# Fused attention and maxout feed-forward on one core: ScalarE's exponential moved ahead of evictions and of the rounding of value products, reciprocals moved within VectorE's order

## The chip, the cores and the metric

One NeuronCore of one Trainium2 chip runs the whole kernel. The metric is the device time of one execution in microseconds, lower is better. The engines are TensorE (PE, with its weight loads as PEld), VectorE (DVE), ScalarE (ACT), GpSimd (POOL) and SyncE (SP, which issues most transfers). Each runs its own instructions in program order and waits on semaphores for the others.

## What is computed

Causal attention with a learned decay, then a maxout feed-forward block (B = 8, H = 8, S = 576, D = 64, 4608 tokens, model width 512, inner width 768):

```python
scores = scale * np.matmul(q, k.transpose(0, 1, 3, 2))
cum = np.cumsum(np.maximum(s, 0.0), axis=-1)
bias = -(cum[:, :, :, None] - cum[:, :, None, :])
scores = np.where(causal, -1000000000.0, scores + np.minimum(bias, 0.0))
scores = scores - np.max(scores, axis=-1, keepdims=True)
attn = np.exp(scores)
attn = attn / (np.sum(attn, axis=-1, keepdims=True) + 1e-09)
x = (attn @ v) ...            # to 4608 x 512
h = np.maximum(np.maximum(x @ w1, x @ w2), x @ w3)
out = h @ w_out
```

## The kernel before

Operands of the large products are kept as a high and a low half (f16 pairs, or rounded f32 pairs for q and k), so each rounding takes two steps: ScalarE writes the high half (`prh` for the probabilities, `xh` for the value products), VectorE subtracts it from the exact value and writes the low half (`prl`, `xl`).

The attention is cut into visits, one for a batch and a pair of heads. The first two batches are visited twice, for query blocks 0 and 1 and then for 2, 3 and 4; every later batch has one visit of five blocks per pair of heads (a stacked visit). A step t is one block of 128 queries of one visit; there are 160. The order of all work is written by hand in the loop at L941, and each engine keeps to it. For step t that loop issues, in this order:

- `probs(t)`, first part: the reciprocal `ri` of the sums (L513, VectorE), then `prh` (L529, ScalarE);
- `highest(t+1)`: the negated row maximum `nm` of the next step's scores (L469 or L474, VectorE);
- `probs(t)`, second part: `prl` (L532, VectorE) and the transposes of both halves (by transfers at L541 and L548, or on TensorE in the first visits);
- `drain()` and `flush()`, then one feed-forward group if one is due (`run_group`);
- `scores(t+2)` on TensorE, into the buffer of step t: there are two score buffers, so `prh` and `prl` of step t must have read theirs;
- `expo(t+1)`: two exponentials with sums (L484) and the scaled sum `se` (L489), ScalarE;
- `drain()` and `flush()` again, then the step's list `todo` of preparatory work (on VectorE the splits L162 and L338, maxima of values L300, low halves of values L362 and of weights L704), more feed-forward groups, and `values` of a finished half of a visit (products `av`, L608).

`pending` holds work that follows a product of TensorE. `out` (in `values`) rounds a value product: L617 on ScalarE and L618 on VectorE. The `ev` of a feed-forward group evicts it: of three groups `pm` (L731, twelve matmuls each) the first goes through ScalarE (L745), the others through VectorE (L748), which take the maximum. The output groups `po` (L773) go through ScalarE (L781), scaled by `os` (L766). `flush` issues GpSimd's split of the result into `hh` and `hl`. When the last pair of heads of a batch is rounded, `add_set` queues the groups of a feed-forward set; how many groups a step issues is set by a running account of TensorE's time (`cost`).

```python
next(parts)
drain()
flush()
if ready() and cost[0] > 0:
    run_group()
...
if t + 1 < len(steps):
    expo(t + 1)
```

Of the kernel before, what the change touches and what calls it, by code (L numbers as in the profile page):

```python
# [8 lines left out]
F32 = mybir.dt.float32  # L9
# [6 lines left out]
ALU = mybir.AluOpType  # L16
# [5 lines left out]
def kernel(  # L22
# [9 lines left out]
    nc = tc.nc  # L32

    P = 128
# [9 lines left out]
    NFT = NW // 4  # L44
    NB = qkv0.shape[0]
# [248 lines left out]
    AM, VS, OS = {}, {}, {}  # L294
# [183 lines left out]
    def expo(t):  # L478
# [11 lines left out]
        SE[t] = (se, nj)  # L490

    PT = {}
    TP = {}
# [6 lines left out]
    def probs(t):  # L500
# [10 lines left out]
        pT = PT[v, ph]  # L511
        ri = small.tile([P, 2], F32, tag="ri", name=f"ri{t}", bufs=3)
        nc.vector.reciprocal(out=ri[:, :nj], in_=se[:, :nj])  # L513
        halves = [att.tile([P, 8, P], F16, tag=f"pr{c}", name=f"pr{c}{t}") for c in "hl"]
# [197 lines left out]

    def drain():
        while pending:
            pending.pop(0)()

    def add_set(b, ph):
# [5 lines left out]

        def h_group(ft, i):
            pm = ps_m.tile([P, 512], F32, tag="m", name=f"pm{u}_{ft}_{i}")
            w = W[3 * ft + i]
# [34 lines left out]
        def o_group(dt):  # L761
            drain()
            flush()
            if dt == 0:
                st["os"] = small.tile([P, 1], F32, tag="os", name=f"os{u}", bufs=2)
                nc.gpsimd.tensor_scalar(  # L766
                    out=st["os"], in0=OS[b, ph if b < NB else 1], scalar1=WS["kw"], scalar2=None, op0=ALU.mult
                )
            pm = ps_m.tile([P, 512], F32, tag="m", name=f"po{u}_{dt}")
# [24 lines left out]
    def flush():  # L794
        while later:
            later.pop(0)()

    def ready():
        return bool(queue) and all(i in W for i in queue[0][1])
# [24 lines left out]

    early = {}

    def soon(t, f, *a):
        early.setdefault(t, []).append((f, a))

    middle = {}  # L830
# [104 lines left out]
    scores(1)  # L935
    expo(0)
    for t in sorted(k for k in todo if k < 0):
        for f, a in todo[t]:
            if f not in (prep2, prep3) or a[0] > 1:
                f(*a)  # L940
    for t, (v, qb) in enumerate(steps):  # L941
# [11 lines left out]
        next(parts)  # L953
        drain()
        flush()
        if ready() and cost[0] > 0:
            run_group()
        for f, a in early.get(t, ()):
            f(*a)
        if t + 2 < len(steps):  # L960
# [7 lines left out]
        for f, a in todo.get(t, ()):  # L968
            f(*a)
        while ready() and cost[0] > 0:  # L970
            run_group()
# [66 lines left out]
```

## Time and profile before

| what | value |
|---|---|
| median of 3 runs (lowest, highest) | 893.19 us (892.27, 893.97) |
| the profiled execution's own time | 893.29 us |
| its span on the engines | 891.5 us |
| TensorE busy, idle | 831.3 us (93%), 60.2 us |
| VectorE busy | 582.6 us (65%) |
| ScalarE busy | 558.9 us (63%) |
| GpSimd busy | 369.3 us (41%) |

The span goes from the first to the last instruction; the 1.8 us between it and the execution's time lie around it. An engine's idle time matters only where another engine, in the end TensorE, waits for it. The waits and the timeline name for an idle stretch the engine and line that ended it.

### The profile page before, as it was taken

To read this page: it belongs to the slowest core of one execution; us is meant where nothing else is said; L and a number is where in the kernel's file an instruction comes from. 1 tells how busy PE (TensorE), PEld (TensorE's weight loads), DVE (VectorE), ACT (ScalarE), POOL (GpSimd) and SP (SyncE) were. 2 spreads that over 40 slices of the span, in tenths; PEclk is the share of its full clock that TensorE was granted. 3 is DMA by queue.
4 is the path that set the end of the run, shared out by engine and by line. 5 is a ranking of instruction groups with operands and counts; after the bars stand their busy time and mean duration, and the time that the engine had idled before them with its cause. 6 is when DMAs were issued, how large, how long until landed. Compare 5 with 4: busy or idle time off the path is not lost. (4 is left out here: it accounts for less than half of the span.)

```text
span 891.5 us, 19856 instructions
## 1 busy us (share of the span) xinstructions
PE 831.3 (93%) x7048; PEld 647.5 (73%) x7048; DVE 582.6 (65%) x1465; ACT 558.9 (63%) x1486; POOL 369.3 (41%) x580
## 2 busy tenths in 40 slices
PE   4878889889999879999999999999999999999998
PEld 2646678766677668777787778877887778777875
DVE  6778877567677667676776767676767676661110
ACT  4567676566677766776768766666767676751111
POOL 5533424223636525455463534455454535221211
PEclk9999999989999979999999999999999999999999
DMA  9722355565986675776767656666657586541000
GB/s 358 271 74 56 100 130 142 132 145 131 195 179 145 162 154 112 165 145 137 167 144 161 148 150 160 154 139 144 160 118 154 144 153 126 94 73 39 13 13 30
DMA packets 233588, 120.75 MB, mean 135 GB/s; under 512 B 209361, under 2 KB 218065, under 8 KB 233489
## 3 DMA queue, kind: packets, MB, share of 16 engines
q1 hardware_dynamic: 232336, 117.65, 56.5%
q10 hardware_dynamic: 1152, 1.84, 0.7%
q8 instruction: 56, 0.92, 0.5%
q14 instruction: 44, 0.35, 0.2%
HBM read 60.18 MB, written 9.44 MB: 78 GB/s over the span
## 5 line engine op out<-in xcount | busy, mean ns | idle before, releaser
L731 PE MATMUL pm<-x,w 128*128 128x256 f16 (+1 forms) x3456 | 453.1, 288 | 3.0 <-DVE x L618 2.1
L731 PEld LDWEIGHTS <-w 128*128 128x128 f16 x3456 | 330.3, 99 | 95.0 <-issue 9.6
L737 POOL CAST hh<-m 128x256 f16<-128x256 f32 (+1 forms) x96 | 54.9, 572 | 347.3 <-DVE m L748 293.8
L529 ACT ACTIVATE prh<-s,ri 128x512 f16<-128x512 f32 (+3 forms) x288 | 142.1, 539 | 84.3 <-DVE ri L513 78.6
L532 DVE SCALAR_TENSOR_TENSOR prl<-s,ri,prh 128x512 f16<-128x512 f32 (+3 forms) x288 | 152.9, 568 | 50.0 <-ACT prh L529 34.9
L748 DVE SCALAR_TENSOR_TENSOR m<-pm,m 128x256 f32<-128x256 f32 (+1 forms) x192 | 87.3, 455 | 134.6 <-PE pm L731 117.4
L484 ACT ACTIVATE s<-s,nm 128x512 f32<-128x512 f32 (+4 forms) x288 | 151.2, 525 | 11.9 <-DVE nm L469 5.0
L773 PE MATMUL po<-hh,w 128*128 128x256 f16 (+1 forms) x768 | 148.9, 286 | 2.2 <-POOL hh L737 2.2
L773 PEld LDWEIGHTS <-w 128*128 128x128 f16 x1152 | 110.1, 98 | 35.1 <-issue 7.3
L469 DVE CUSTOM_DVE_ANT_0 s<-s,later 128x128 f32<-128x128 f32 (+1 forms) x192 | 94.5, 492 | 30.2 <-PE s L391 26.9
L773 PE MATMUL po<-hl,w 128*128 128x320 f16 (+1 forms) x384 | 109.7, 286 | 2.0 <-POOL hl L738 1.9
L745 ACT ACTIVATE m<-pm 128x256 f32<-128x256 f32 (+1 forms) x96 | 39.2, 408 | 92.3 <-PE pm L731 91.8
L738 POOL TENSOR_TENSOR hl<-m,hh 128x256 f16<-128x256 f32 (+1 forms) x96 | 74.8, 779 | 7.8
L781 ACT ACTIVATE o<-po,os 128x256 f32<-128x256 f32 (+1 forms) x64 | 31.9, 499 | 70.1 <-PE po L773 57.5
L171 POOL TENSOR_TENSOR l<-raw,h 64x576 fp32r<-64x576 f32 x48 | 67.8, 1413 | 13.1 <-ACT h L157 11.6
L474 DVE TENSOR_REDUCE nm<-s 128x1 f32<-128x576 f32 (+3 forms) x64 | 49.9, 779 | 23.8 <-PE s L433 9.6
L140 POOL CAST l<-kb 64x576 fp32r<-64x576 f32 x48 | 33.0, 688 | 74.3 <-PE s L402 68.7
L391 PE MATMUL s<-h 128*128 128x128 f32 (+1 forms) x192 | 54.9, 368 | 7.6 <-ACT se L489 2.6
L608 PEld LDWEIGHTS <-vh 128*64 128x64 f16 x832 | 47.5, 116 | 19.0 <-issue 11.6
L484 ACT ACTIVATION_READ_ACCUMULATOR s<-s,nm 128x1 f32 x288 | 57.3, 199 | 0.0
L608 PE MATMUL av<-ph,vh 128*64 128x320 f16 (+3 forms) x384 | 53.6, 296 | 0.3 <-DMA ph<-prh 0.3
L617 ACT ACTIVATE x<-av 128x256 f16<-128x256 f32 (+1 forms) x64 | 26.2, 410 | 36.9 <-PE av L608 35.6
(145 smaller groups left out, 1091.3 us busy)
## 6 DMA issues: line engine op xcount, KB each, us to landing
raw<-in_qk_dram SPq DMA_DIRECT2D x48, 608.0 KB, 4.6
r<-in_w_dram SPq DMA_DIRECT2D x24, 512.0 KB, 10.2
rv<-in_qkv_dram SPq DMA_DIRECT2D x32, 320.0 KB, 3.2
out_dram<-o SPq DMA_DIRECT2D x32, 160.0 KB, 2.0
out_dram<-o SPq DMA_DIRECT2D x32, 128.0 KB, 2.1
raw<-in_qkv_dram SPq DMA_DIRECT2D x8, 480.0 KB, 3.8
ph<-prh SPq DMA_TRANSPOSE x184, 2.9
pl<-prl SPq DMA_TRANSPOSE x184, 2.6
```

What stands on the lines that cost most here:

```text
L171: nc.gpsimd.tensor_tensor(out=l[far, QP:V0], in0=raw[far, QP:V0], in1=h[far, QP:V0].bitcast(F32), op=ALU.subtract)
L391: nc.tensor.matmul(ps[:, j, :nk], lhsT=w[:, qs], rhs=w[:, QP:QP + nk], start=(x == "h"), stop=(x == "l"), skip_group_check=True,)
L469: nc.vector.tensor_tensor_reduce(out=sc[:, j], in0=sc[:, j], in1=future[0][:, Q4 - nk:Q4], scale=-1.0, scalar=3.0e38, op0=ALU.add, op1=ALU ...
L484: nc.scalar.activation(out=sc, in_=sc, func=AF.Exp, bias=nm[:, j:j + 1], scale=-1.0 if below(t) else 1.0, accum_out=sm[:, j:j + 1],)
L529: nc.scalar.activation(out=hi, in_=src, func=AF.Copy, scale=sc)
L532: nc.vector.scalar_tensor_tensor(out=lo, in0=src, scalar=sc, in1=hi, op0=ALU.mult, op1=ALU.subtract)
L608: nc.tensor.matmul(av[j * D:(j + 1) * D, c0:nq], lhsT=lt, rhs=rt, start=(n < 2), stop=(n >= len(todo) - 2), skip_group_check=True,)
L731: nc.tensor.matmul(pm[:, :nq], lhsT=w[:, wt, kt, :], rhs=xt, start=(n == 0), stop=(n == 3 * NKT - 1))
L737: nc.gpsimd.tensor_copy(out=st["hh"][:, ft, :nq], in_=m1[:, :nq])
L738: nc.gpsimd.tensor_tensor(out=st["hl"][:, ft, :nq], in0=m1[:, :nq], in1=st["hh"][:, ft, :nq], op=ALU.subtract)
L748: nc.vector.scalar_tensor_tensor(out=m1[:, :nq], in0=pm[:, :nq], scalar=HSC, in1=m1[:, :nq], op0=ALU.mult, op1=ALU.max)
L773: nc.tensor.matmul(pm[:, :nq], lhsT=W[18 + ft][:, wt, dt, :], rhs=st[ht][:, ft, :nq], start=(n == 0), stop=(n == 3 * NFT - 1),)
```

## The change

`drain` gets an argument, how many entries to leave, and stops at an `out`. The drain ahead of `scores(t+2)` and `expo(t+1)` leaves the last eviction and each `out` in `pending`, and the flush there is gone; both are issued by the drain behind `expo(t+1)`. The reciprocal leaves `probs`: a new function `inverse(t+1)` issues it in step t, behind the first entry of `todo` that works on VectorE (`on_vector`), or behind the whole list. The scale `os` is computed with the last feed-forward group of a set rather than with the first output group, and only the first output group drains and flushes. An unused list (`early`, `soon`) goes.

```diff
+    RI = {}
+    def inverse(t):
+        se, nj = SE[t]
+        RI[t] = small.tile([P, 2], F32, tag="ri", name=f"ri{t}", bufs=3)
+        nc.vector.reciprocal(out=RI[t][:, :nj], in_=se[:, :nj])
...
-        ri = small.tile([P, 2], F32, tag="ri", name=f"ri{t}", bufs=3)
-        nc.vector.reciprocal(out=ri[:, :nj], in_=se[:, :nj])
+        ri = RI.pop(t)
...
-    def drain():
-        while pending:
+    def drain(left=0):
+        while len(pending) > left and not (left and pending[0].__name__ == "out"):
             pending.pop(0)()
...
         def h_group(ft, i):
+            if (ft, i) == (NFT - 1, 0):
+                st["os"] = small.tile([P, 1], F32, tag="os", name=f"os{u}", bufs=2)
+                nc.gpsimd.tensor_scalar(
+                    out=st["os"], in0=OS[b, ph if b < NB else 1], scalar1=WS["kw"], scalar2=None, op0=ALU.mult
+                )
...
         def o_group(dt):
-            drain()
-            flush()
             if dt == 0:
-                st["os"] = small.tile([P, 1], F32, tag="os", name=f"os{u}", bufs=2)
...
+                drain()
+                flush()
...
+    on_vector = (vmax, vscale2, prep3, prep5, head_qlo, decode2, decode4, gram2, wscale2)
...
     expo(0)
+    inverse(0)
...
         next(parts)
-        drain()
-        flush()
+        drain(1 + sum(f.__name__ == "out" for f in pending))
         if ready() and cost[0] > 0:
             run_group()
...
         for f, a in todo.get(t, ()):
             f(*a)
+            if f in on_vector and t + 1 < len(steps) and t + 1 not in RI:
+                inverse(t + 1)
+        if t + 1 < len(steps) and t + 1 not in RI:
+            inverse(t + 1)
```

What this does to the order of each engine, at three places. In the rows of the changed kernel the lines behind the edit have other numbers: L535 is L529 of before, L538 is L532, L623 and L624 are L617 and L618, L742 is L731, L756 and L759 are L745 and L748; the reciprocal (L513) is L497.

ScalarE, steps 46 to 48 (a stacked visit's query blocks 1 to 3; `x16_1` is the rounded second value product of the visit before, `pm1_1_3_0` a feed-forward group). Before:

```order
L529 ACTIVATE prh46_3897<-s46_3780,ri46_3895 128x2x128 x2
L617 ACTIVATE x16_1_3907<-av16_1_3866 128x320
L484 ACTIVATE s47_3842,sm47_3929<-s47_3842,nm47_3843 128x384 x2
L489 ACTIVATE se47_3932<-sm47_3929 128x2
L157 ACTIVATE h18_1_3859<-raw18_1_3719 128x576
L529 ACTIVATE prh47_3957<-s47_3842,ri47_3955 128x3x128 x2
L745 ACTIVATE m11_1_3_3967<-pm1_1_3_0_3940 128x320
L484 ACTIVATE s48_3923,sm48_3993<-s48_3923,nm48_3924 128x512 x2
L489 ACTIVATE se48_3996<-sm48_3993 128x2
```

and with the change:

```order
L535 ACTIVATE prh46_3897<-s46_3779,ri46_3855 128x2x128 x2
L484 ACTIVATE s47_3840,sm47_3926<-s47_3840,nm47_3841 128x384 x2
L489 ACTIVATE se47_3929<-sm47_3926 128x2
L623 ACTIVATE x16_1_3931<-av16_1_3868 128x320
L157 ACTIVATE h18_1_3861<-raw18_1_3719 128x576
L535 ACTIVATE prh47_3957<-s47_3840,ri47_3940 128x3x128 x2
L484 ACTIVATE s48_3920,sm48_3991<-s48_3920,nm48_3921 128x512 x2
L489 ACTIVATE se48_3994<-sm48_3991 128x2
L756 ACTIVATE m11_1_3_3996<-pm1_1_3_0_3942 128x320
```

The rounding `x16_1` stood between `prh46` and the exponential of step 47 and now stands behind that exponential; the eviction of the first group of three moved from ahead of the exponential of step 48 to behind it. Of the 63 roundings that stood between a `prh` and the next exponential, 61 moved like this one.

TensorE, the first feed-forward set (`av3_0` is the last value product that the set needs, `pm0_0_0_0` to `_2` its first three groups, `s10` the scores of a step two ahead, `gmv1_0` a small product for the next values' scale; of each run of equal matmuls one or two rows are shown). Before:

```order
L608 MATMUL av3_0_834<-pl6_717,vh3_691 64x128
L731 MATMUL pm0_0_0_0_863<-x0_0_433,w0_779 128x256
L427 MATMUL s10_876<-qkh5_768 128x128 x2
L433 MATMUL s10_876<-tri_99,identb_98 128x128
L291 MATMUL gmv1_0_902<-identb_98,ambv1_0_900 128x128
L731 MATMUL pm0_0_0_1_915<-x0_0_433,w0_779 128x256
L731 MATMUL pm0_0_0_2_928<-x0_0_433,w1_782 128x256
```

and with the change:

```order
L614 MATMUL av3_0_836<-pl6_719,vh3_693 64x128
L427 MATMUL s10_861<-qkh5_770 128x128 x2
L433 MATMUL s10_861<-tri_99,identb_98 128x128
L291 MATMUL gmv1_0_889<-identb_98,ambv1_0_887 128x128
L742 MATMUL pm0_0_0_0_902<-x0_0_452,w0_781 128x256
L742 MATMUL pm0_0_0_1_915<-x0_0_452,w0_781 128x256
L742 MATMUL pm0_0_0_2_928<-x0_0_452,w1_784 128x256
```

The first group stood ahead of the scores and now stands behind them and behind the small product. The same happens at three later sets.

VectorE, steps 20 and 21 (`qkl10` is a split of the queries and keys of a later visit). Before:

```order
L362 SCALAR_TENSOR_TENSOR vl9_1831<-rv9_1116,inv0_1_1763,vh9_1830 128x640
L338 SCALAR_TENSOR_TENSOR qkl10_1918<-raw10_1590,qkh10_1838 128x384
L513 RECIPROCAL ri20_1952<-se20_1910 128x2
L474 TENSOR_REDUCE nm21_1897<-s21_1896 128x1
L532 SCALAR_TENSOR_TENSOR prl20_1955<-s20_1808,ri20_1952,prh20_1954 128x4x128 x2
L618 SCALAR_TENSOR_TENSOR x8_1_1963<-av8_1_1923,x8_1_1963 128x320
```

and with the change:

```order
L362 SCALAR_TENSOR_TENSOR vl9_1831<-rv9_1118,inv0_1_1748,vh9_1830 128x640
L497 RECIPROCAL ri20_1916<-se20_1909 128x2
L338 SCALAR_TENSOR_TENSOR qkl10_1920<-raw10_1590,qkh10_1840 128x384
L474 TENSOR_REDUCE nm21_1896<-s21_1895 128x1
L538 SCALAR_TENSOR_TENSOR prl20_1955<-s20_1807,ri20_1916,prh20_1954 128x4x128 x2
L624 SCALAR_TENSOR_TENSOR x8_1_1992<-av8_1_1925,x8_1_1992 128x320
```

The reciprocal of step 20 stood behind the split and now stands ahead of it. In 32 of the 160 steps the reciprocal moves in such a way, in the others it stays where it was.

## Rows read from the trace of the kernel before

**Rows 1.** The profile's page, its part on busy time: microseconds, share of the span and number of instructions of each engine.

```profile
PE 831.3 (93%) x7048; PEld 647.5 (73%) x7048; DVE 582.6 (65%) x1465; ACT 558.9 (63%) x1486; POOL 369.3 (41%) x580
```

**Rows 2.** Busy time by stretch of the span: the stretch, its length, then busy time (and instructions) of PE, PEld, DVE, ACT and POOL, the granted clock of TensorE (1.00 is full), the DMA engines' share and GB/s.

```profile
340.00:880.00 540.00, 532.35 (x4619) 421.75 (x4616) 337.59 (x902) 334.58 (x894) 230.48 (x369) 1.00 0.57 124
```

**Rows 3.** All waits of the execution, by the engine and line that waited and what released it: total microseconds, times, the longest.

```profile
DVE m L748 <- PE pm L731: 117.4, 90, 11.7
ACT m L745 <- PE pm L731: 91.8, 58, 4.5
...
ACT x L617 <- PE av L608: 35.6, 35, 4.6
...
PE s L427 <- DVE prl L532: 6.4, 3, 3.4
...
PE s L402 <- DVE prl L532: 5.6, 6, 3.2
...
PE pm L731 <- DVE x L618: 2.1, 3, 0.8
```

**Rows 4.** Groups of instructions of ScalarE by line and shape: count | busy microseconds, mean nanoseconds of one | idle time before them.

```profile
L484 ACT ACTIVATION_READ_ACCUMULATOR s<-s,nm 128x1 f32 x288 | 57.3, 199 | 0.0
...
L484 ACT ACTIVATE s<-s,nm 128x384 f32<-128x384 f32 x64 | 35.5, 554 | 1.4 <-DVE nm L474 0.2
...
L489 ACT ACTIVATE se<-sm 128x2 f32<-128x2 f32 x128 | 26.1, 204 | 4.1
```

**Rows 5.** The timeline of one step of a stacked visit (the first such visit, its query blocks 1 to 4): start, duration, engine, line, what it does, in brackets the idle time before it and what ended it.

```profile
272.06 0.44 ACT L617 ACTIVATE x<-av 128x320 f16<-128x320 f32 x1
272.33 0.14 DVE L469 DVE_READ_ACCUMULATOR2_ANT nm<- 128x1 f32 x1
...
272.51 0.56 ACT L484 ACTIVATE s<-s,nm 128x384 f32<-128x384 f32 x1
...
273.12 0.48 DVE L618 SCALAR_TENSOR_TENSOR x<-av,x 128x320 f16<-128x320 f32 x1
...
273.78 0.49 DVE L748 SCALAR_TENSOR_TENSOR m<-pm,m 128x320 f32<-128x320 f32 x1 [0.18 <-PE pm L731]
...
274.31 0.82 DVE L162 SCALAR_TENSOR_TENSOR h<-raw,h 64x640 fp32r<-64x640 f32 x1
...
274.51 3.43 PE L731 MATMUL pm<-x,w 128*128 128x320 f16 x24
...
275.24 0.68 DVE L469 CUSTOM_DVE_ANT_0 s<-s,later 128x512 f32<-128x512 f32 x1
...
276.63 1.14 DVE L532 SCALAR_TENSOR_TENSOR prl<-s,ri,prh 128x384 f16<-128x384 f32 x2
...
277.92 0.48 PE L402 MATMUL s<-h 128*128 128x256 f32 x2
```

**Rows 6.** The timeline of the same step in the last such visit, same columns.

```profile
692.08 0.48 DVE L618 SCALAR_TENSOR_TENSOR x<-av,x 128x320 f16<-128x320 f32 x1
...
693.90 0.70 DVE L469 CUSTOM_DVE_ANT_0 s<-s,later 128x512 f32<-128x512 f32 x1 [0.30 <-PE s L391]
...
695.31 1.14 DVE L532 SCALAR_TENSOR_TENSOR prl<-s,ri,prh 128x384 f16<-128x384 f32 x2
...
696.87 0.51 PE L402 MATMUL s<-h 128*128 128x256 f32 x2
```

**Rows 7.** The timeline around the first feed-forward set, same columns.

```profile
64.55 2.23 PE L731 MATMUL pm<-x,w 128*128 128x256 f16 x10
...
66.62 0.61 DVE L532 SCALAR_TENSOR_TENSOR prl<-s,ri,prh 128x128 f16<-128x128 f32 x2
...
67.14 0.42 DVE L618 SCALAR_TENSOR_TENSOR x<-av,x 128x256 f16<-128x256 f32 x1
...
67.61 0.38 PE L731 MATMUL pm<-x,w 128*128 128x256 f16 x2 [0.84 <-DVE x L618]
...
69.86 0.25 PE L291 MATMUL gmv<-identb,ambv 128*128 128x128 bf16 x1 [1.06 <-DVE ambv L287]
```

**Rows 8.** Busy time by stretch at the same place, columns as in rows 2.

```profile
66.50:69.90 3.40, 1.50 (x15) 0.87 (x14) 3.37 (x11) 3.05 (x10) 0.00 (x0) 1.00 0.17 39
70.00:73.30 3.30, 3.30 (x17) 2.33 (x16) 2.09 (x5) 2.69 (x9) 0.00 (x0) 0.50 0.41 109
```

**Rows 9.** The timeline around the fourth feed-forward set, columns as in rows 5.

```profile
326.09 1.26 PE L731 MATMUL pm<-x,w 128*128 128x256 f16 x10
...
326.21 1.41 DVE L532 SCALAR_TENSOR_TENSOR prl<-s,ri,prh 128x512 f16<-128x512 f32 x2 [0.28 <-ACT prh L529]
...
328.00 0.38 PE L731 MATMUL pm<-x,w 128*128 128x256 f16 x2 [0.65 <-DVE x L618]
```

**Rows 10.** Single rows of the timeline at three other places where TensorE waits or a chain is late, same columns.

```profile
101.87 0.88 DVE L532 SCALAR_TENSOR_TENSOR prl<-s,ri,prh 128x256 f16<-128x256 f32 x2 [0.58 <-ACT prh L529]
...
102.89 0.39 PE L427 MATMUL s<-qkh 64*128 64x256 f32 x2 [3.40 <-DVE prl L532]
...
139.47 1.41 DVE L532 SCALAR_TENSOR_TENSOR prl<-s,ri,prh 128x512 f16<-128x512 f32 x2 [0.68 <-ACT prh L529]
...
159.63 0.38 ACT L745 ACTIVATE m<-pm 128x256 f32<-128x256 f32 x1 [1.70 <-PE pm L731]
...
164.19 1.14 DVE L532 SCALAR_TENSOR_TENSOR prl<-s,ri,prh 128x384 f16<-128x384 f32 x2 [0.75 <-ACT prh L529]
```

More of the change, by code (lines that the diff above doesn't have):

```diff
@@ L761, in o_group @@
         def o_group(dt):
-            drain()
-            flush()
             if dt == 0:
-                st["os"] = small.tile([P, 1], F32, tag="os", name=f"os{u}", bufs=2)
-                nc.gpsimd.tensor_scalar(
-                    out=st["os"], in0=OS[b, ph if b < NB else 1], scalar1=WS["kw"], scalar2=None, op0=ALU.mult
-                )
+                drain()
+                flush()
             pm = ps_m.tile([P, 512], F32, tag="m", name=f"po{u}_{dt}")
@@ L823 @@
     todo = {}
-    early = {}
-    def soon(t, f, *a):
-        early.setdefault(t, []).append((f, a))
+    on_vector = (vmax, vscale2, prep3, prep5, head_qlo, decode2, decode4, gram2, wscale2)
     middle = {}
@@ L953 @@
         next(parts)
-        drain()
-        flush()
+        drain(1 + sum(f.__name__ == "out" for f in pending))
         if ready() and cost[0] > 0:
             run_group()
-        for f, a in early.get(t, ()):
-            f(*a)
         if t + 2 < len(steps):
```

## The prediction, made before the changed kernel ran

> **What bounds the kernel now.** I read the page's busy times first, then the stretches, then the waits, then the timeline of the places that the waits name. TensorE is busy 93% of the span, VectorE 65% and ScalarE 63% [rows 1]. After 340 us TensorE works 532.35 of 540 us at the full granted clock [rows 2]; before that it stands still here and there. So a microsecond counts only if TensorE loses or gains it. ScalarE waits long for TensorE ahead of an eviction (91.8 us at L745) and ahead of a rounding of value products (35.6 us at L617), and in program order the next exponential stands behind both; that is what the change attacks. But TensorE itself waits for the chain of scores, maximum, exponential, reciprocal, `prh`, `prl` only 6.4 + 5.6 = 12.0 us in all [rows 3]. That is all there is to win on this chain.
>
> Times are reckoned against the profiled run, 893.29 us, of which the span is 891.5. The median of the three runs is 893.19, 0.1 us less.
>
> **What moves, and the rule of its cost.** TensorE may write the scores of step t+2 only when `prl` of step t, on VectorE, has read the buffer. VectorE runs in program order. Of the change only two things reach it: the reciprocal moves in 32 of 160 steps, and the second half of a rounding (L618) must wait until ScalarE has done the first half (L617), which now comes after the exponential. Where VectorE reaches L618 before that, all behind it waits too: evictions, split, the next maximum, the next `prl`.
>
> *Steady part, loss.* The exponential of a 128x384 block takes 2 x 0.554 on ScalarE, 2 x 0.199 for the sums and 0.204 for the scaled sum, some 1.6 us with the starts [rows 4]. In the step shown, ScalarE ran L617 at 272.06, while VectorE was still at the maximum, whose last part ended at 272.33 + 0.14 = 272.47; the exponential followed at 272.51 [rows 5]. So L617 sat in a hole: moving it lets the exponential start 0.04 sooner, nothing more. Now L617 starts at about 274.06 and ends 0.44 later, at 274.5. L618 ran at 273.12, so it comes 1.4 late. Of that the wait of 0.18 ahead of the eviction at 273.78 is absorbed, and from there VectorE has no idle time up to `prl` at 276.63: eviction, split, reciprocal and maximum stand end to end. `prl` ends at 277.77 + 1.2, and the scores, which started at 277.92, 0.15 after it (0.14 stands between the two at 102.89 too, where TensorE did wait for `prl` [rows 10], so it isn't slack), come 1.2 late: **+1.2**. TensorE has no other work in its program order there: the 24 matmuls ahead end at 277.94 [rows 5].
>
> In the last such step L618 at 692.08 comes 1.4 late, the maximum at 693.90 had waited 0.30 for scores and other small idle time takes 0.1, so `prl` comes 1.0 late; its end, 696.45, left 0.28 of slack beyond the 0.14 until the scores at 696.87: +0.7 [rows 6]. I did this at every rounding. Ten of the stacked visits lose, the first and the last as shown, the others between 0.1 and 1.1: together **+5.8**. At the other roundings of the stacked part TensorE finished the value products so late that L618 had waited for L617 anyway, or VectorE waits for TensorE behind it; there I cost the move at nothing. If that cover (117.4 us of VectorE waiting for groups of L731 [rows 3]) were thinner, each would cost up to the same 1.2; if the 0.14 and 0.15 were slack, the ten would cost 4.3.
>
> *First groups of the sets.* In three sets the first group, whose last two matmuls need the last rounding, waited for it 2.1 us in all [rows 3]. That group now stands behind the scores of t+2. At the first set 2.23 us of it ran from 64.55 while `prl` (66.62, 0.61) was still to come. Now TensorE idles from 64.6 until the scores can start at 67.4, and again, behind the scores, until the small product L291 at 69.86, which comes some 0.9 later, since VectorE gets to L618 0.9 later (ScalarE's exponential first) [rows 7]. Idle time grows from 0.84 + 1.06 to about 5.3, by 3.4 us. Before, the stretch behind that idle time ran at a granted clock of 0.50, the lower of the two levels (1.2 against 2.4 GHz), 3.3 us shown, all of it work [rows 8]; I take it that the lower level now falls into the longer idle time, which gives back half of 3.3: 3.4 - 1.65 = **+1.75**, between that and 3.4 without anything given back. At the second set the idle time grows by 1.0 but the scores come 0.5 sooner, and VectorE waits for them: **+0.5** (0 to 1.0). At the fourth, 1.26 us of the group at 326.09 filled the time until `prl` ended at 327.62; now 1.7 us stand empty in place of 0.65: **+1.0** [rows 9]. The third set's group does not gain an empty stretch: nothing.
>
> *Gains.* At 101.87 and 139.47 `prl` waited 0.58 and 0.68 for `prh`, which waited for a reciprocal behind a maximum of values or a split (L300, L338). The reciprocal now goes ahead of them, and its own 0.16 leaves the chain in the first case: **-0.7** and **-0.7**. At 159.63 an eviction waited 1.70 for TensorE in front of an exponential; with the exponential first, `prh` comes a microsecond sooner and `prl` at 164.19 loses its wait: **-0.75** [rows 10].
>
> *Costed at nothing.* The early roundings of the first 60 us delay only copies that wait for ScalarE anyway. The scale `os` moves a few instructions ahead on POOL (busy 41% [rows 1]) into time in which it waits. The three moved transfers of output on SP go to a queue whose work no engine waits for there. Evictions behind the exponential free their buffer up to 1.6 us later; there are three such buffers, and the groups that need them are paced apart by more.
>
> **Sum:** 5.8 + 1.75 + 0.5 + 1.0 - 0.7 - 0.7 - 0.75 = +6.9, and 893.29 + 6.9 = **900.2 us**.
>
> **A rule against this sum.** In the row shown 24 matmuls of 320 columns take 3.43 us, 143 ns each, end to end [rows 5], so I see no room in TensorE to catch up a late start. The Trainium skill, Perfetto Trace Analysis, Identifying the Most-Contended Engine, holds that matmul busy time is a poor measure of headroom and that the weight loads' busy share is a better one. By that share, 73%, TensorE would have room, the steady loss would be made up, and the sum would be 1.1 instead of 6.9; the row speaks against it.
>
> **The rivals.**
>
> *Faster.* VectorE absorbs the late roundings (the idle time I could not see in single places is there, as its 35% idle share [rows 1] suggests), and the chain gains wherever TensorE waited for it. The place that decides is the one at 277.92: if the scores start no later there, the steady loss is nothing. Gains shown sum to 2.15; if half of the 12.0 us of rows 3 goes, 6.0. The middle, 4, gives 889.3 us. For it: 91.8 us of waits ahead of exponentials end. Against it: VectorE stands without a gap there, and ScalarE is not the bound.
>
> *No change.* The losses at sets and the steady ones are absorbed, and the gains too, because later waits end when TensorE does: 893.5 us. That most rows move within idle time of engines speaks for it. That the change does little (32 of 160 reciprocals move) belongs here as well.
>
> *Slower still, by the clock.* If at the first set the half clock does not fall into idle time, that costs 1.65 more, and if the new empty stretches at the second and the fourth set each bring another stretch like it, twice 1.65 again: 900.2 + 4.95 = 905.2. The Trainium skill, TensorE: Matmul & The Clock Gate, HAM oscillation, describes the same thing: waits of TensorE end in work at the low clock. Here the trace agrees at one place: idle time of 0.84 and 1.06, then the stretch at 0.50 [rows 7, 8].
>
> **How the numbers follow.** Forecast 0.48, slower still 0.10, no change 0.17, faster 0.25. What measurement can tell from no change is about 0.2%, 1.8 us: below 891.4 counts as faster, above 895.0 as slower. So slower 0.58, same 0.17, faster 0.25. The range from 889 to 905 takes in the forecast, its bounds and most of the rivals; the forecast's own range is 897 (the ten at 4.3, the first set's and the fourth's cost half made up) to 903 (the first set at 3.4, the second at 1.0, another rounding without cover).
>
> **What would show it.** Right: VectorE's waits for L617, ahead of L618, more than double; in the ten steps the scores of the fifth block start later against the groups ahead of them, with a gap on TensorE of about 0.3 to 1.2; the first set shows some 5 us of idle TensorE; the waits at 101.87 and 139.47 are gone. ScalarE's wait at L617 for value products falls well under 35.6. TensorE's busy time stays near 831 and the idle time grows by some 7 us. Wrong: if no new gap of TensorE stands in front of scores in the stacked visits, the steady term fails; if TensorE's idle time before 340 us shrinks by over 3 us, the chain was worth more than I gave it; if the first set's idle time does not grow, the moved group found other cover.

## The result, and the profile after

The changed kernel takes 901.32 us (median of 4 runs, 900.95 to 903.1) against 893.02 (892.27 to 893.97): ratio 1.0094, 95% interval 1.0078 to 1.011. It is slower by about 8.4 us, on the side that was forecast and 1.1 us above the forecast of 900.2. The sum was made of terms, and some of them were wrong in ways that made up for each other; that is what the experiments are for.

The profiled execution of the changed kernel has a span of 899.2 us, 7.7 more than before. Its page, in the columns of [rows 1], shows the other engines about as busy as before. TensorE's busy time fell from 831.3 us to 825.8, and its idle time grew from 60.2 us to 73.4; so the time went into waiting:

```profile
PE 825.8 (92%) x7048; PEld 643.9 (72%) x7048; DVE 584.3 (65%) x1465; ACT 559.5 (62%) x1486; POOL 370.5 (41%) x580
```

The waits, in the columns of [rows 3] (L623 and L624 are the two halves of a rounding, L538 is `prl`, L535 `prh`). First two lines of before:

```profile
DVE x L618 <- ACT x L617: 15.5, 16, 2.1
...
PE s L391 <- DVE prl L532: 1.5, 3, 0.7
```

and with the change:

```profile
DVE x L624 <- ACT x L623: 32.3, 29, 2.0
...
DVE prl L538 <- ACT prh L535: 22.4, 37, 2.5
...
PE s L402 <- DVE prl L538: 9.2, 11, 3.1
...
PE s L427 <- DVE prl L538: 9.0, 5, 2.7
...
ACT x L623 <- PE av L614: 7.3, 6, 4.4
...
PE s L391 <- DVE prl L538: 4.0, 4, 1.7
```

ScalarE's waits for value products ahead of a rounding fell from 35.6 us to 7.3, as the change intends. VectorE's waits for ScalarE's half of a rounding grew from 15.5 us to 32.3. And TensorE's waits for `prl` ahead of the scores at L402, L427 and L391, before 5.6 + 6.4 [rows 3] + 1.5 = 13.5, are now 9.2 + 9.0 + 4.0 = 22.2.

The step of [rows 5] in the changed kernel, same columns:

```profile
273.77 0.14 DVE L469 DVE_READ_ACCUMULATOR2_ANT nm<- 128x1 f32 x1
...
273.94 0.56 ACT L484 ACTIVATE s<-s,nm 128x384 f32<-128x384 f32 x1 [0.34 <-DVE nm L469]
...
275.46 0.42 ACT L623 ACTIVATE x<-av 128x320 f16<-128x320 f32 x1
...
275.91 0.49 DVE L624 SCALAR_TENSOR_TENSOR x<-av,x 128x320 f16<-128x320 f32 x1 [1.27 <-ACT x L623]
...
276.32 0.48 DVE L759 SCALAR_TENSOR_TENSOR m<-pm,m 128x320 f32<-128x320 f32 x1
276.83 0.82 DVE L162 SCALAR_TENSOR_TENSOR h<-raw,h 64x640 fp32r<-64x640 f32 x1
...
277.75 0.68 DVE L469 CUSTOM_DVE_ANT_0 s<-s,later 128x512 f32<-128x512 f32 x1
...
279.14 1.14 DVE L538 SCALAR_TENSOR_TENSOR prl<-s,ri,prh 128x384 f16<-128x384 f32 x2
...
280.42 0.47 PE L402 MATMUL s<-h 128*128 128x256 f32 x2 [1.04 <-DVE prl L538]
```

The exponential starts 0.03 us after the maximum's last part (273.77 + 0.14); before, it came 0.04 after it, with the rounding already done. So it gained nothing. VectorE, ready for the second half of the rounding at 274.64, waits 1.27 for the first half, and the eviction, the split, the maximum and `prl` follow one another without idle time. `prl` ends at 280.28, and TensorE has waited 1.04 for it.

The first feed-forward set, where [rows 7, 8] stood before: single rows of the timeline, and busy time by stretch in the columns of [rows 2].

```profile
66.53 0.47 PE L427 MATMUL s<-qkh 64*128 64x128 f32 x2 [2.66 <-DVE prl L538]
...
69.88 0.29 PE L291 MATMUL gmv<-identb,ambv 128*128 128x128 bf16 x1 [1.91 <-DVE ambv L287]
...
69.96 2.34 PE L742 MATMUL pm<-x,w 128*128 128x256 f16 x10
```

```profile
48.30:63.80 15.50, 9.01 (x65) 5.47 (x65) 10.79 (x33) 8.98 (x25) 4.22 (x6) 0.50 0.18 52
63.90:69.80 5.90, 1.44 (x10) 1.06 (x10) 5.25 (x14) 5.43 (x15) 0.00 (x0) 0.50 0.21 50
69.90:75.50 5.60, 5.60 (x27) 3.99 (x28) 1.74 (x5) 1.82 (x8) 0.00 (x0) 0.50 0.23 56
```

TensorE waits 2.66 us ahead of the scores and 1.91 ahead of the small product. Before, it waited 0.84 ahead of the group's last matmuls and 1.06 ahead of the small product. The granted clock is at its lower level from before this place until 75.5, through 5.6 us in which TensorE works without a break.

Two places where the reciprocal gains, [rows 10] before:

```profile
103.29 0.86 DVE L538 SCALAR_TENSOR_TENSOR prl<-s,ri,prh 128x256 f16<-128x256 f32 x2
...
104.30 0.39 PE L427 MATMUL s<-qkh 64*128 64x256 f32 x2 [2.66 <-DVE prl L538]
```

```profile
141.09 1.41 DVE L538 SCALAR_TENSOR_TENSOR prl<-s,ri,prh 128x512 f16<-128x512 f32 x2
```

`prl` no longer waits for `prh` at either; the first gap of TensorE shrank from 3.40 to 2.66.

### The profile page after: what moved, and what is told of

Read it like the earlier page. It is cut to its first block, busy times and chain, and to the rows that moved or that the text cites. A ratio compares the mean times of both kernels' runs of the same rounds, so it can differ in the third digit from the quotient of the medians.

```text
span 899.2 us, 19842 instructions
## 1 busy us (share of the span) xinstructions
PE 825.8 (92%) x7048; PEld 643.9 (72%) x7048; DVE 584.3 (65%) x1465; ACT 559.5 (62%) x1486; POOL 370.5 (41%) x580
## 5 line engine op out<-in xcount | busy, mean ns | idle before, releaser
L742 PE MATMUL pm<-x,w 128*128 128x256 f16 (+1 forms) x3456 | 452.8, 288 | 0.7 <-DVE m L759 0.7
L742 PEld LDWEIGHTS <-w 128*128 128x128 f16 x3456 | 331.1, 99 | 92.2 <-issue 6.1
L535 ACT ACTIVATE prh<-s,ri 128x512 f16<-128x512 f32 (+3 forms) x288 | 142.4, 540 | 97.3 <-DVE ri L497 93.3
L748 POOL CAST hh<-m 128x256 f16<-128x256 f32 (+1 forms) x96 | 54.8, 571 | 355.1 <-DVE m L759 304.6
L759 DVE SCALAR_TENSOR_TENSOR m<-pm,m 128x256 f32<-128x256 f32 (+1 forms) x192 | 87.3, 455 | 141.5 <-PE pm L742 123.6
L538 DVE SCALAR_TENSOR_TENSOR prl<-s,ri,prh 128x512 f16<-128x512 f32 (+3 forms) x288 | 152.8, 567 | 37.6 <-ACT prh L535 22.4
L756 ACT ACTIVATE m<-pm 128x256 f32<-128x256 f32 (+1 forms) x96 | 38.9, 406 | 82.0 <-PE pm L742 81.8
L171 POOL TENSOR_TENSOR l<-raw,h 64x576 fp32r<-64x576 f32 x48 | 67.8, 1412 | 11.6 <-ACT h L157 10.2
L140 POOL CAST l<-kb 64x576 fp32r<-64x576 f32 x48 | 35.0, 729 | 75.0 <-PE s L402 69.7
L391 PE MATMUL s<-h 128*128 128x128 f32 (+1 forms) x192 | 54.8, 367 | 10.1 <-DVE prl L538 4.0
L614 PEld LDWEIGHTS <-vh 128*64 128x64 f16 x832 | 45.7, 113 | 19.9 <-issue 13.8
L614 PE MATMUL av<-ph,vh 128*64 128x320 f16 (+3 forms) x384 | 51.6, 288 | 0.2 <-PE s L407 0.2
L624 DVE SCALAR_TENSOR_TENSOR x<-av,x 128x256 f16<-128x256 f32 (+1 forms) x64 | 29.1, 455 | 33.3 <-ACT x L623 32.3
```

The lines of the kernel that those rows point to most:

```text
L171: nc.gpsimd.tensor_tensor(out=l[far, QP:V0], in0=raw[far, QP:V0], in1=h[far, QP:V0].bitcast(F32), op=ALU.subtract)
L391: nc.tensor.matmul(ps[:, j, :nk], lhsT=w[:, qs], rhs=w[:, QP:QP + nk], start=(x == "h"), stop=(x == "l"), skip_group_check=True,)
L535: nc.scalar.activation(out=hi, in_=src, func=AF.Copy, scale=sc)
L538: nc.vector.scalar_tensor_tensor(out=lo, in0=src, scalar=sc, in1=hi, op0=ALU.mult, op1=ALU.subtract)
L614: nc.tensor.matmul(av[j * D:(j + 1) * D, c0:nq], lhsT=lt, rhs=rt, start=(n < 2), stop=(n >= len(todo) - 2), skip_group_check=True,)
L742: nc.tensor.matmul(pm[:, :nq], lhsT=w[:, wt, kt, :], rhs=xt, start=(n == 0), stop=(n == 3 * NKT - 1))
```

## The experiments

Every ratio is against runs of the kernel before on the same chip in the same series (medians 890.5 to 892.6 us there), so that ratios, not times, are compared between series; a difference in microseconds is the ratio's, times 892.6. For the places where time goes, the traces of two kernels are compared step by step: the start of the scores of step t+2 in the one less that in the other, and where this difference jumps. Each trace is of one execution. `...` in code marks lines left out.

| kernel | ratio to before | 95% interval | us |
|---|---|---|---|
| the change | 1.0094 | 1.0078 to 1.011 | +8.4 |
| reciprocals sooner alone | 0.9964 | 0.9949 to 0.9979 | -3.2 |
| the change, reciprocals in their old place | 1.0132 | 1.0111 to 1.0153 | +11.8 |
| the change, roundings ahead | 0.9964 | 0.9948 to 0.998 | -3.2 |
| the change, evictions ahead | 1.0081 | 1.0068 to 1.0094 | +7.2 |
| the change, set-closing roundings ahead | 1.0028 | 1.0009 to 1.0048 | +2.5 |
| only set-closing roundings behind | 1.0080 | 1.0059 to 1.010 | +7.1 |
| VectorE's half later, closing ones ahead | 1.0007 | 0.9995 to 1.0019 | +0.6 |
| new order from step 40 only | 1.0069 | 1.0055 to 1.0082 | +6.2 |
| only 18 steady roundings behind | 1.0011 | 0.9994 to 1.0027 | +1.0 |
| only the first set's rounding behind | 0.9999 | 0.9983 to 1.0015 | -0.1 |
| only the third and fourth set's behind | 1.0036 | 1.0021 to 1.005 | +3.2 |
| roundings ahead, evictions behind to step 39 | 0.9945 | 0.9929 to 0.9961 | -4.9 |

**Which part of the change costs the time?** Four kernels took it apart. Reciprocals sooner, in the kernel before (`inverse`, `RI` and `on_vector` as in the change):

```diff
 # in probs(t)
-        ri = small.tile(...)
-        nc.vector.reciprocal(out=ri[:, :nj], in_=se[:, :nj])
+        ri = RI.pop(t)
...
 # in the loop over todo
             f(*a)
+            if f in on_vector and t + 1 < len(steps) and t + 1 not in RI:
+                inverse(t + 1)
+        if t + 1 < len(steps) and t + 1 not in RI:
+            inverse(t + 1)
```

> The kernel before with the reciprocals sooner on VectorE and nothing else of the change. Theory (the loss comes from the roundings behind the exponential, the reciprocals only gain): the waits of prl for prh at 101.87 and 139.47 go, 0.7 us each, so 893.0 - 1.4 = 891.6 us. Rival A (the reciprocals, waiting for ScalarE ahead of splits and maxima, hold up VectorE): 896 us or more. Rival B (evictions behind the exponential are the cost): as the theory, 891.6.

The change with the reciprocals back behind all splits:

```diff
 # in probs(t)
+        inverse(t)
         ri = RI.pop(t)
...
 # in the loop over todo
             f(*a)
-            if f in on_vector and t + 1 < len(steps) and t + 1 not in RI:
-                inverse(t + 1)
-        if t + 1 < len(steps) and t + 1 not in RI:
-            inverse(t + 1)
```

> The change with the reciprocals back in their old place, behind all splits. Theory: loses the 1.4 us that the reciprocals gain, so 901.3 + 1.4 = 902.7 us. Rival A (reciprocals are the cost): 896 us or less.

The change with the roundings ahead of the exponential:

```diff
-        drain(1 + sum(f.__name__ == "out" for f in pending))
+        rounded = [f for f in pending if f.__name__ == "out"]
+        pending[:] = [f for f in pending if f.__name__ != "out"]
+        drain(1)
+        for f in rounded:
+            f()
```

> The change with the roundings of value products back ahead of the exponential; the last eviction stays behind it, the reciprocals stay sooner. Theory: the first groups of the sets stand ahead of the scores again, the steady loss is gone, all gains stay: 893.0 - 0.7 - 0.7 - 0.75 = 890.9 us. Rival B (the evictions behind the exponential come late to VectorE's maximum and GpSimd): 897 us or more.

The change with all evictions ahead of the exponential, and only the roundings behind it:

```diff
-        drain(1 + sum(f.__name__ == "out" for f in pending))
+        rounded = [f for f in pending if f.__name__ == "out"]
+        pending[:] = [f for f in pending if f.__name__ != "out"]
+        drain()
+        flush()
+        pending[:] = rounded
```

> The change with all evictions back ahead of the exponential; only the roundings stay behind it, the reciprocals stay sooner. Theory: all losses stay and the gain at 165 us goes: 901.3 + 0.75 = 902.1 us. Rival B (evictions are the cost): 896 us or less.

The roundings are the cost: with them ahead the time is 3.2 us below that of before, with them behind it is 7.2 above whatever the evictions do (the interval of the kernel with evictions ahead overlaps that of the change, so the 0.75 us expected of them isn't seen). The reciprocals are a gain, alone and in the change (3.2 and 3.4 us), and a larger one than the 1.4 expected. Both rivals, reciprocals and evictions as the cost, are out.

**Sets or the steady part?** Only the 16 roundings that close a set (the last pair of heads) ahead, or only these behind; `out.closes` is `g == NP - 1`. In the first of the two, an eviction that is pending at such a step goes ahead with the rounding:

```diff
 # set-closing roundings ahead
         drain(1 + sum(f.__name__ == "out" for f in pending))
+        if any(getattr(f, "closes", False) for f in pending):
+            drain()
+            flush()
```

> The change with only those roundings back ahead of the exponential that close a feed-forward set (the last pair of heads, 16 of 64), so that each set's first group stands ahead of the scores as before. The other 48 roundings stay behind. With all roundings ahead the kernel took 889.6 us, with all behind 901.3. Theory (both the sets and the steady part lose): the steady part stays, 5.8 by my sum less the few of the ten steps that close a set, so 894 to 895 us. Rival A (all of the loss is at the sets, by idle time and half clock): 890 us. Rival B (all of it is steady): 900 us.

```diff
 # only set-closing roundings behind
-        drain(1 + sum(f.__name__ == "out" for f in pending))
+        rounded = [f for f in pending if f.__name__ == "out"]
+        pending[:] = [f for f in pending if f.__name__ != "out"]
+        drain(1)
+        for f in rounded:
+            if f.closes:
+                pending.append(f)
+            else:
+                f()
```

> The opposite: only the 16 roundings that close a set stay behind the exponential, the 48 others go ahead of it again. Theory: 889.6 us and the cost of the sets, 3.25 by my sum (1.75 + 0.5 + 1.0), 6 to 7 by the shifts that the trace of the change shows at the sets, so 893 to 896.5 us. Rival A (sets are all): 901. Rival B (steady is all): 890 us.

Both lose, so neither rival (all at the sets, all steady) holds. Against the kernel with all roundings ahead the 48 roundings that close nothing cost 5.7 us and the 16 that close a set 10.3, more than expected; the two don't add up to the 11.6 that all of them cost together. The trace of the second shows only some 4.8 us of it, and its profiled execution was the fastest of six, 893.62 against a median of 896.86. The sets one by one, further down, bear the 10.3 out: 3.1 for the first and 6.4 for the third and fourth. Why the sets and the other roundings together cost less than the two alone stays open.

The new order from step 40 on only:

```diff
-        drain(1 + sum(f.__name__ == "out" for f in pending))
+        if t < FROM:            # FROM = 40
+            drain()
+            flush()
+        else:
+            drain(1 + sum(f.__name__ == "out" for f in pending))
```

> The change with evictions and roundings in the order of before in steps 0 to 39 (up to some 258 us) and in the new order from step 40, the stacked visits. Reciprocals sooner everywhere. Theory: 889.6 us with the steady loss of 5 to 6 and the last of the four sets' empty stretches (1.0 by my sum, 2.4 by the trace): 895.5 to 898 us. Rival (the loss comes from the first 200 us, where the granted clock of the change is low for long): 890 to 891 us.

+6.2, more than was expected (the ratio makes 899.2 us of the 893.0 before): the larger part of the loss lies in steps 40 and later, and the rival, that the first 200 us with their low clock make it, is out.

**Is it VectorE's wait, and how large is the steady part alone?** In the kernel with set-closing roundings ahead, VectorE's half of the other roundings of the stacked visits was moved behind the step's list (against the change, without the lines that put the set-closing roundings ahead):

```diff
-            nc.vector.scalar_tensor_tensor(out=xl, ...)
+            def low():
+                nc.vector.scalar_tensor_tensor(out=xl, ...)
+            if stacked(v) and g < NP - 1:
+                lows.append(low)
+            else:
+                low()
...
 # in the loop, behind todo and inverse(t + 1)
+        while lows:
+            lows.pop(0)()
```

> As the kernel with set-closing roundings ahead, but in the stacked visits VectorE's half of the other roundings (the subtraction) stands behind the step's list of preparatory work and the reciprocal, so that VectorE never waits for ScalarE's half, which stays behind the exponential. Theory (the steady loss is VectorE waiting in order for the late first half): the loss goes, 889 to 890 us, and the gaps ahead of the fifth block's scores at about 279 and 490 us are gone. Rival (ScalarE's later work behind the exponential is late in itself, or the scores wait for something else): no change against that kernel, 894 to 895 us.

The ratio fell from 1.0028 to 1.0007, a third of the 5.7 us. That is neither the theory (all of it) nor the rival (nothing). The step of [rows 5] in that kernel, same columns (L768 evicts, L623 and L626 are the rounding):

```profile
268.28 0.49 DVE L768 SCALAR_TENSOR_TENSOR m<-pm,m 128x320 f32<-128x320 f32 x1 [0.58 <-PE pm L751]
...
268.53 0.42 ACT L623 ACTIVATE x<-av 128x320 f16<-128x320 f32 x1
...
269.66 0.17 DVE L497 RECIPROCAL ri<-se 128x2 f32<-128x2 f32 x1
269.74 0.47 DVE L626 SCALAR_TENSOR_TENSOR x<-av,x 128x320 f16<-128x320 f32 x1
...
271.53 1.14 DVE L538 SCALAR_TENSOR_TENSOR prl<-s,ri,prh 128x384 f16<-128x384 f32 x2
...
272.81 0.36 PE L402 MATMUL s<-h 128*128 128x256 f32 x1 [0.36 <-DVE prl L538]
```

L626 starts without a wait and `prl` and the scores are late by less: 0.36 us of waiting in place of 1.04. What is left is most likely the 0.47 of L626 itself, which no run took out alone. It stood in a stretch in which VectorE would wait for TensorE anyway (the eviction L768 now waits 0.58 there, 0.18 in [rows 5]) and now stands where VectorE is the bound. In the comparison of the traces four such jumps of 1.08, 0.64, 1.00 and 0.65 became 0.39, 0, 0.40 and 0, while two at other steps grew from 0.18 to 0.39. So VectorE's wait is what makes these four, and the fix gives a part of it back.

Only the 18 roundings of second halves that close no set, in the kernel with all others ahead (the code of the kernel above, with `f.behind` in place of `f.closes`):

```diff
+        out.behind = stacked(v) and ph == 1 and g < NP - 1
```

> The kernel with all roundings ahead of the exponential (0.9964 of the time before), with only the 18 roundings behind it that belong to the second halves of stacked visits and close no set. My sum for these of the ten steps: 1.2 + 0.3 + 0.1 + 0.8 + 1.1 + 0.3 + 0.7 = 4.5, so 1.3 us above the time before. The trace of the change, against that of the kernel with all ahead, shows 1.07 + 0.64 + 1.01 + 0.66 = 3.4 at four of them: 0.2 us above. Rival (the steady part costs nothing, all is at the sets): 3.2 us below the time before.

+1.0 us, 4.2 above its base, between the two expectations and with an interval that takes in both; the rival is out. The place of the first such step shows the same wait as in the change:

```profile
274.82 0.47 PE L402 MATMUL s<-h 128*128 128x256 f32 x2 [1.05 <-DVE prl L538]
```

**How large are the sets one by one?**

```diff
+        out.behind = g == NP - 1 and (b, ph) == (0, 0)                # the first set
+        out.behind = g == NP - 1 and (b, ph) in ((0, 1), (2, 0))      # third and fourth
```

> The same base with only the rounding behind the exponential that closes the first feed-forward set. My sum: +1.75 (3.4 of idle time less half of a half-clock stretch), so 1.4 us below the time before. If nothing is given back, as the trace of the change shows (+3.8): 0.6 us above it. Rival (the idle time is absorbed before 100 us): 3.2 below.

The first set alone costs 3.1 us against its base (-0.1 against before), with an interval from 1.7 to 4.5 (the base at its own ratio); my 1.75 is at its edge. The 3.8 that the expectation takes from the trace of the change is the jump at one step. The scores one step earlier had come 0.6 us sooner there, since the group no longer stood ahead of them, so that trace too shows about 3.1. Its two waits, same columns as before, are those of the change:

```profile
65.83 0.48 PE L427 MATMUL s<-qkh 64*128 64x128 f32 x2 [2.67 <-DVE prl L538]
...
69.18 0.29 PE L291 MATMUL gmv<-identb,ambv 128*128 128x128 bf16 x1 [1.91 <-DVE ambv L287]
```

> The same base with only the two roundings behind the exponential that close the third and the fourth set whose first group moved. My sum: 0 + 1.0, so 2.2 us below the time before. The trace of the change: 2.6 + 2.3 = 4.9 with their half-clock stretches, so 1.7 us above it. Rival (nothing): 3.2 below.

+3.2, 6.4 above its base: my sum, 1.0, is refuted, and so is the rival; the trace's 4.9 lies below the interval (5.1 to 7.7) too. This kernel's own trace shows 1.4 us at the third set and 3.1 at the fourth. Where it goes at the fourth set is seen in the stretches behind it. First the kernel with roundings ahead, then the one with these two behind, with the row of the scores:

```profile
318.90:322.20 3.30, 3.30 (x24) 2.25 (x23) 2.31 (x4) 3.02 (x7) 2.85 (x6) 0.50 0.26 59
322.30:325.60 3.30, 3.30 (x32) 3.02 (x31) 2.90 (x10) 2.63 (x9) 0.60 (x1) 1.00 0.85 165
```

```profile
323.10:326.40 3.30, 1.76 (x16) 1.39 (x13) 3.02 (x5) 2.35 (x7) 2.81 (x5) 0.50 0.46 102
326.50:329.80 3.30, 3.30 (x17) 2.32 (x16) 1.77 (x8) 1.68 (x6) 0.00 (x0) 0.50 0.93 215
```

```profile
325.27 0.66 PE L391 MATMUL s<-h 128*128 128x128 f32 x2 [1.53 <-DVE prl L538]
```

With the roundings ahead TensorE is busy through both stretches, and the second runs at full clock. With them behind, TensorE idles 1.53 us, and the stretch behind that, all of it work, runs at 0.50: 17 instructions in 3.3 us in place of 32. The wait costs its own length less what it replaces, and here then half of a stretch of work.

The half is not paid each time. In the kernel with only the 16 set-closing roundings behind, the scores' row at the same place and the stretch behind it are:

```profile
325.62 0.41 PE L391 MATMUL s<-h 128*128 128x128 f32 x2 [1.62 <-DVE prl L538]
...
327.30:330.60 3.30, 3.30 (x33) 2.94 (x31) 2.11 (x7) 1.98 (x8) 0.00 (x0) 1.00 0.89 227
```

After a wait of 1.62 us the work ran at full clock, and the fourth set cost 0.9 us. In the traces of the six kernels in which this group moved, TensorE waited 1.5 to 1.9 us for `prl` there. The place cost 0.8 and 0.9 us in the two in which the clock was full behind the wait, and 2.1 to 3.1 in the four in which it was half.

**The fastest version.** Evictions behind the exponential helped one of the first 40 steps and, in the trace of the kernel with all roundings ahead, cost 0.43 and 0.63 us at two steps of the stacked visits. So: roundings ahead, reciprocals sooner, evictions behind only in the first 40 steps.

```diff
-        drain(1)
+        drain(1 if t < 40 else 0)
+        if t >= 40:
+            flush()
```

> All roundings ahead and reciprocals sooner; the last eviction behind the exponential in steps 0 to 39 only, ahead of it in the stacked visits. If evictions behind the exponential cost 0.43 + 0.63 us in the stacked visits, as two steps of the trace suggest: 4.2 us below the time before, the fastest here. If they cost nothing, as the equal medians of reciprocals alone and of all roundings ahead suggest: 3.2 below.

0.9945, 4.9 us below the time before: the fastest kernel here. Its intervals and those of the two kernels at 0.9964 overlap a little, so that it beats them is likely and not certain.

## Why the prediction was right, and what in it was not

The direction and the total were right: 900.2 forecast, 901.3 measured, slower with the largest chance. The total owes part of that to chance. The prediction wanted TensorE's busy time to stay near 831 us and its idle time to grow by some 7. In the profiled executions the idle time grew by 13.2, and the busy time fell by 5.5: less of TensorE's work before 345 us ran at half clock (55 us of work against 70).

By its steps, with the change compared to the kernel with all roundings ahead (only the roundings' place differs), and for the gains to the kernel before:

| step of the prediction | forecast | by the traces |
|---|---|---|
| steady, step of [rows 5] | +1.2 | +1.07 |
| steady, last such step [rows 6] | +0.7 | +0.66 |
| steady, the other eight | 3.9 in sum | 0.64, 1.01, 0.25, 0.26 at four of them, nothing at four |
| first set [rows 7, 8] | +1.75 | +3.1 |
| second set | +0.5 | +0.8 |
| third set | 0 | +2.6 |
| fourth set [rows 9] | +1.0 | +2.3 |
| gains at 100, 140 and 165 us [rows 10] | -0.7, -0.7, -0.75 | -0.75, -0.66, -0.84 |

*The steady part.* The mechanism was right, and at six of ten steps the size too, within 0.2. At the four others, 1.3 us in my sum, TensorE lost nothing: the lateness that I carried through VectorE's order to the scores did not reach them. So 3.9 of 5.8 us came. At each of two more steps the change lost 0.56 less than the kernel it is compared with here, whose evictions cost 0.4 and 0.6 there.

*The sets.* Here the forecast was far too low, 3.25 against 8.8. Two sentences of it failed. "The third set's group does not gain an empty stretch": before, the scores there started 2.3 us after `prl` had ended, because value products and the first group were still running; without the group ahead TensorE waits for `prl`, and in this execution the work behind it runs at the lower clock. (In the kernel with the third and fourth set's roundings behind, TensorE waits the same 0.93 us there, the clock behind is full, and the place costs 1.4 us in place of 2.6.) Two stretches and the scores' row of the change at that place:

```profile
184.90:188.20 3.30, 1.02 (x15) 0.89 (x15) 1.82 (x4) 1.05 (x4) 0.00 (x0) 1.00 0.54 141
188.20:191.60 3.40, 3.40 (x18) 2.05 (x16) 1.69 (x6) 2.59 (x5) 0.00 (x0) 0.50 0.69 157
```

```profile
187.94 0.46 PE L427 MATMUL s<-qkh 64*128 64x384 f32 x2 [0.93 <-DVE prl L538]
```

And "the lower level now falls into the longer idle time, which gives back half of 3.3": it does fall into the idle time, but it lasts through the work behind it all the same, 5.6 us at the first set where it was 3.3 before. Nothing is given back there; in this execution 3.4 and 3.2 us of work behind the waits at the third and fourth set ran at half clock as well. That was the rival "slower still, by the clock", to which I gave 0.10: its mechanism is seen at three of four places. The Trainium skill, TensorE: Matmul & The Clock Gate, HAM oscillation, tells of longer waits, for transfers, behind which the next work starts at the low clock. These rows agree, with waits of 0.93 to 2.66 us, and the kernel with full clock behind 1.62 us shows that it need not happen.

Over the whole execution the clock took nothing: in the kernel with all roundings ahead TensorE was busy for 826.2 us and idle for 60.7, in the change 825.8 and 73.4. The half-clock work behind the sets' waits was made up by work elsewhere before 345 us that ran at full clock in this execution (55 us of work at half clock in all, against 58). So the loss against that kernel is idle time, and how much the clock adds on average stays open.

*The gains.* The three that were reckoned came, each within 0.1. But reciprocals alone gained 3.2 us and not the 1.4 of the two of them that are its own: in its trace, of the fastest of twelve executions, further jumps of 0.3 to 1.5 stand between 170 and 330 us, at places where I had counted no wait for a reciprocal. Stretches at half clock fall differently there in the two traces, so how much of this is the reciprocals' own chain stays open. The "faster" rival was right in this much. These, and the missing four steady steps, made up for the sets; the total came out near for that reason. The prediction's bound of 12.0 us on what this chain can give left out 1.5 us of such waits at L391 and 0.8 at L448.

*What no step of the prediction has.* Against the kernel before, three more jumps stand in the trace of the change: -1.6 and -1.9 us at the scores of 173 and 188 us, where the kernel before ran work at half clock and the change did not, and +1.4 at 222 us, where TensorE waited 1.49 us for a transfer of `prl`. The last section shows that such a wait comes and goes without any change of order.

*The rule weighed against the sum.* The Trainium skill, Perfetto Trace Analysis, Identifying the Most-Contended Engine, takes the share of weight loads, rather than matmul busy time, as a measure of TensorE's headroom. From it I reckoned, as the other outcome, that the steady loss would be made up. Where `prl` came late without slack it was not: +1.01 at the scores of 493 us and +0.66 at those of 705 us stayed to the end.

*The costs put at nothing.* Evictions behind the exponential cost nothing in sum, by the equal ratios of reciprocals alone and of all roundings ahead, with 0.4 and 0.6 us at two steps against 0.8 gained at 165 us. No jump stands at the scale on GpSimd or at the three transfers on SP. The early roundings before 60 us cost nothing: the scores of steps 5 to 8 came 1.2 to 1.3 us sooner. That is not shown to be their doing, since the traces of three kernels in which these roundings stand as before (reciprocals alone, only the first set's, only the third and fourth set's behind) show 1.4 to 1.5 there.

## What to carry to other kernels

Before moving work behind a longer piece on one engine, look at whether it sat in a hole there: if it did, nothing is gained, and the engine that does its second half in program order waits for all of the longer piece. A short operation on which another engine waits (here a reciprocal of 0.16 us) is worth moving ahead of long ones that nobody waits for. And price a new wait of TensorE with the work behind it, which may run at half clock in one execution and not in the next (here 0.8 to 3.1 us for a wait of 1.5 to 1.9), before counting it at its length.

## What was not expected of the hardware

The stretches at half clock don't fall in the same places in every execution, even where the work is the same. Two kernels whose orders are the same up to step 40, some 245 us (all roundings ahead, and the same with evictions ahead from step 40) show it at 114 us, in one execution each; columns as in [rows 2]. All roundings ahead:

```profile
110.50:113.90 3.40, 1.54 (x15) 1.13 (x12) 3.40 (x6) 0.72 (x2) 0.37 (x1) 1.00 0.25 51
114.10:117.30 3.20, 2.96 (x26) 2.42 (x27) 1.82 (x4) 3.14 (x9) 0.82 (x1) 1.00 0.69 182
```

and the fastest kernel:

```profile
110.50:113.90 3.40, 1.51 (x14) 1.11 (x12) 3.40 (x6) 0.72 (x2) 0.35 (x1) 1.00 0.25 52
114.10:117.30 3.20, 2.98 (x14) 2.05 (x15) 1.11 (x4) 3.14 (x8) 0.84 (x1) 0.50 0.67 181
```

After the same idle time, 1.54 and 1.51 us busy of 3.40, the next stretch ran at full clock in the one, with 26 instructions, and at 0.50 in the other, with 14; the scores behind it came 1.4 us later.

Transfers vary as well. The kernel with 18 steady roundings behind also has the order of all roundings ahead up to step 40. In the trace of all roundings ahead the last value products of one visit start without a wait:

```profile
211.67 1.04 PE L614 MATMUL av<-pl,vh 128*64 128x320 f16 x9
```

and in the other kernel's TensorE waits for the transfer of `prl` in front of them:

```profile
214.24 0.65 PE L614 MATMUL av<-pl,vh 128*64 128x320 f16 x8 [1.28 <-DMA pl<-prl]
```

The scores behind it came 1.2 us later. Such differences may be a good part of why 23 executions of the kernel before lie between 890.0 and 897.7 us on one chip; no run measured how much. So a jump of 1 to 2 us between two single traces in the first 330 us is no evidence by itself. Of those at the sets, the first set's (2.8 to 3.3 us) and the second's (0.8) are of much the same size in every trace that has them, the other two are not.
